# Filler matmuls from a table, and a new order of all work, in attention with a two-layer block

## The chip, the cores and the metric

The kernel runs on one core of one Trainium2 chip. The metric is the time of one execution in device microseconds, as the median of several runs. Five engines work side by side and wait for each other by semaphores: TensorE (PE), VectorE (DVE), ScalarE (ACT), GpSimd (POOL) and SyncE (SP), which issues most of the transfers.

## What is computed

Attention with a band and block sums (4 batches, 8 heads, 768 rows, 64 columns), and on its output a two-layer block over 3,072 rows (512 to 2,048 to 512):

```python
k_sum = k.reshape(B, H, nb, block, D).max(axis=3)      # block = 32
v_sum = v.reshape(B, H, nb, block, D).mean(axis=3)
scores_l = scale * np.matmul(q, k.transpose(0, 1, 3, 2))
mask_l = np.abs(pos[:, None] - pos[None, :]) < window   # window = 16
scores_s = scale * np.einsum('bhsd,bhnd->bhsn', q, k_sum) + np.log(block)
...
a = a / (np.sum(a, axis=-1, keepdims=True) + 1e-09)
return np.matmul(a, np.concatenate([v, v_sum], axis=2))
# then, on x = the heads side by side:
h = x @ w_in
g = h - np.tanh(h)
return g @ w_out
```

## The kernel before

The rows are cut into eight units `u` of 384 rows (two to a batch), the heads into two groups `g` of four. For a unit and a group the work runs: loads of k, q and v; turns of k and q on VectorE into `kT` and `qT`; block maxima of k (`top`) and their copy between the keys (`top put`); block means of v by matmuls (`sum`), copied out and put among the v rows by transfers (`mean put`); `scores` on TensorE; for each pair of heads a softmax (`min` on VectorE, `exp` on ScalarE, `inverse`, `normal`); turns of the probabilities on TensorE (`p turn`) and their copies out (`p out`); `values`; and then the layers: `in`, the activation (`tanh`, `square`, `series`, `g`, split into `g high` and `g low`), `out`. Weights come as 64-bit numbers and are converted by VectorE and ScalarE (`w scale` to `w sign`). The probabilities lie in three buffers (`PROBS`, line 24), so the next pair's `min` waits for turns of the pair before.

Every piece of work is a task of a `Plan`. The plan has 3,628 tasks with a number each. `ORDER` (line 29) is a list of these numbers, found by a search beforehand, that fixes the order in which all tasks are issued, and so each engine's own order. `ON` (line 32) is a letter for each task that tells its engine where several could do it (D, A, P, S; T for TensorE). `Plan.follow` walks through ORDER, books each task on its engine with a written-out cost, and follows TensorE's clock by a small model (`Clock`).

`follow` also puts in fillers. A filler is a matmul of the 128x128 identity by itself that nobody reads (`keep_warm`, near the end of `program`); it occurs as two records in the trace. Where the plan expects TensorE to wait, it fills the expected gap with fillers of a booked cost of 0.111 us:

```python
while spot < 2 and now - free[PE] > 2 * cost + 0.1:
    d = Task()
    d.after, d.order, d.go, d.engine, d.start = (), (), go[spot], PE, free[PE]
    d.out = free[PE] = clock.run(free[PE], cost)
```

`spot` is 0 up to the second scores (the fillers write the bank `pY2`), 1 from the first values to the third scores (they write `pS0`), and 2 later: no fillers. An engine works its tasks strictly in order, so whatever stands behind a filler on TensorE waits for it. The start of TensorE's order is: sum 0, sum 1, scores 0, p turn 0 to 2, scores 1 (the second group of the same unit, from the buffers `wg3` and `oo`), p turn 3 to 5, values 0, the first steps of `in`, and so on to scores 2, the next unit's.

Of the kernel before, what the change touches and what calls it, by code (L numbers as in the profile page):

```python
# [1335 lines left out]
```

## Time and profile before

| | us |
|---|---|
| median of 3 runs | 671.39 |
| lowest and highest | 670.67, 675.03 |
| the profiled execution | 673.41 |
| its span, first to last instruction | 671.7 |

The profile's page gives the busy time of each engine, its share of the span, a chain of waits followed back from the last instruction, and the costliest groups of instructions. Nearly all instructions are recorded by one helper, so they all have line 55, and the tiles' names tell them apart: `ident` by `ident` is a filler, `kT,qT` into four banks are scores (`wg,oo` the second group's), `ident,prob` are probability turns, `probT,vw` values, `o,wf` the first layer, `gh` by `wf`, `wh` or `wl` into `pY` the second. PEclk is the granted TensorE clock, in tenths of full speed in the page and as a fraction in the windows; the DMA share is the mean busy share of 16 DMA engines. Matmuls are pipelined, so the sum of their durations can be longer than the time they take together, and a few records can be missing.

### The profile page before, as it was taken

To read this page: it belongs to the slowest core of one execution; us is meant where nothing else is said; L and a number is where in the kernel's file an instruction comes from. 1 tells how busy PE (TensorE), PEld (TensorE's weight loads), DVE (VectorE), ACT (ScalarE), POOL (GpSimd) and SP (SyncE) were. 2 spreads that over 40 slices of the span, in tenths; PEclk is the share of its full clock that TensorE was granted. 3 is DMA by queue.
4 is the path that set the end of the run, shared out by engine and by line. 5 is a ranking of instruction groups with operands and counts; after the bars stand their busy time and mean duration, and the time that the engine had idled before them with its cause. 6 is when DMAs were issued, how large, how long until landed. Compare 5 with 4: busy or idle time off the path is not lost.

```text
span 671.7 us, 15484 instructions
## 1 busy us (share of the span) xinstructions
PE 650.4 (97%) x5471; PEld 551.4 (82%) x5471; DVE 450.6 (67%) x1272; ACT 453.6 (68%) x1371; POOL 158.6 (24%) x253
## 2 busy tenths in 40 slices
PE   6999999999799999999999999999999999999997
PEld 6986556678688889988888789989888899999885
DVE  2369899999699775545667894545678863354553
ACT  2169789899698885545588975446598855434774
POOL 2001130104400431331335501322233301000231
PEclk9999999999899999999999999999999999999999
DMA  7737887764686678757625246646553045554101
GB/s 201 191 109 215 226 241 228 195 212 140 190 292 243 213 241 225 235 170 204 201 64 179 74 144 202 199 143 207 158 149 104 22 147 178 177 167 161 47 1 50
DMA packets 120737, 113.26 MB, mean 169 GB/s; under 512 B 45008, under 2 KB 88528, under 8 KB 120656
## 3 DMA queue, kind: packets, MB, share of 16 engines
q1 hardware_dynamic: 116752, 109.61, 53.7%
q10 hardware_dynamic: 3904, 2.62, 1.3%
q8 instruction: 44, 0.72, 0.5%
q14 instruction: 37, 0.30, 0.1%
HBM read 88.87 MB, written 20.97 MB: 164 GB/s over the span
## 4 chain that ended last, share of the span: by engine, by line
PE 68%; DVE 9%; DMA 8%; ACT 6%; POOL 3%; issue 2%; SPq 2%; ACTq 0%; DVEq 0%; POOLq 0%
PE pY L55 34%; PE pH L55 29%; PE pS L55 3%; PE pX L55 2%; DVE tmp L55 2%; DVE wraw L55 2%; SPq L55 2%; ACT prob L55 2%; POOL tmp L55 2%; DMA wraw<-scr 2%; DMA tmp<-in_v_dram 1%; DMA raw<-in_k_dram 1%; DVE prob L55 1%; DMA raw<-in_q_dram 1%; ACT o L55 1%
## 5 line engine op out<-in xcount | busy, mean ns | idle before, releaser
L55 ACT ACTIVATE prob<-prob,stat 128x120 f32<-128x120 f32 x301 | 110.9, 387 | 46.5 <-DVE stat L55 45.8
L55 PE MATMUL pY<-wl,gh 128*128 128x512 f32 x288 | 113.3, 393 | 0.0
L55 PE MATMUL pH<-wf,wraw 128*128 128x384 f32 x552 | 112.4, 338 | 0.9 <-DMA wraw<-scr 0.7
L55 PEld LDWEIGHTS pH<-wf,wraw 128*128 128x128 f32 x552 | 97.4, 188 | 6.9 <-issue 1.4
L55 PE MATMUL pH<-wg,wraw 128*128 128x384 f32 x432 | 85.9, 339 | 1.4 <-DVE o L55 0.9
L55 PE MATMUL pY<-wh,gh 128*128 128x512 f32 x204 | 83.1, 408 | 0.0
L55 PE MATMUL pY<-wh,gl 128*128 128x512 f32 x204 | 80.7, 396 | 0.0
L55 PEld LDWEIGHTS pH<-wg,wraw 128*128 128x128 f32 x432 | 75.7, 188 | 5.9 <-DVE o L55 1.4
L55 PE MATMUL pY<-wg,gh 128*128 128x512 f32 x168 | 69.1, 411 | 0.0
L55 PE MATMUL pH<-o,wf 128*128 128x384 f32 x188 | 66.0, 445 | 2.7 <-DVE wf L55 1.6
L55 ACT ACTIVATE gu<-gu 128x384 f32<-128x384 f32 x128 | 65.6, 520 | 2.0
L55 PE MATMUL pY<-wg,gl 128*128 128x512 f32 x168 | 66.7, 397 | 0.0
L55 PEld LDWEIGHTS pY<-wl,gh 128*128 128x128 f32 x288 | 54.2, 188 | 9.3 <-issue 0.2
L55 POOL TENSOR_TENSOR gl<-gu,gh 128x384 fp32r<-128x384 f32 x28 | 29.2, 1043 | 120.8 <-ACT gh L55 78.9
L55 ACT ACTIVATE gt<-gu 128x384 f32<-128x384 f32 x48 | 25.0, 520 | 39.1 <-DVE gu L55 37.3
L55 PEld LDWEIGHTS pH<-o,wf 128*128 128x128 f32 x188 | 34.6, 191 | 17.9 <-ACT gu L55 1.5
L55 ACT ACTIVATE gv<-pH 128x384 f32<-128x384 f32 x37 | 18.1, 489 | 40.8 <-PE pH L55 40.8
L55 PEld LDWEIGHTS pY<-wh,gl 128*128 128x128 f32 x204 | 38.2, 187 | 8.7
L55 PE MATMUL pY<-wf,gh 128*128 128x512 f32 x108 | 44.8, 439 | 0.0
L55 POOL TENSOR_TENSOR gu<-gu,gt 128x384 f32<-128x384 f32 x24 | 24.4, 1019 | 83.6 <-ACT gu L55 60.6
L55 PEld LDWEIGHTS pY<-wh,gh 128*128 128x128 f32 x204 | 38.4, 188 | 7.0 <-issue 0.3
L55 DVE COPY gv<-pH 128x384 f32<-128x384 f32 x35 | 19.5, 556 | 34.1 <-PE pH L55 34.0
(211 smaller groups left out, 1435.5 us busy)
## 6 DMA issues: line engine op xcount, KB each, us to landing
wraw<-scr SPq DMA_DIRECT2D x72, 512.0 KB
wraw<-in_moe_w_in_dram SPq DMA_DIRECT2D x16, 512.0 KB
wraw<-in_moe_w_out_dram SPq DMA_DIRECT2D x16, 512.0 KB
scr<-wraw SPq DMA_DIRECT2D x16, 512.0 KB
wraw<-scr SPq DMA_DIRECT2D x24, 256.0 KB
raw<-in_q_dram SPq DMA_DIRECT2D x54, 96.0 KB
vw<-in_v_dram SPq DMA_DIRECT2D x60, 80.0 KB
raw<-in_k_dram SPq DMA_DIRECT2D x48, 96.0 KB
```

The lines of the kernel that those rows point to most:

```text
L55: return lambda *args, **kwargs: self._tc.keep_in_program_order(op(*args, **kwargs))
```

## The change

A table `FILL` says before which task how many fillers stand, 37 in all; the old rule for gaps stays only as the branch without a table, and there fills 0.55 of a gap. The cost that is booked for a filler goes from 0.111 to 0.223 us, the rate booked for loads of q and k from 260 to 240 thousand bytes per us. ORDER and ON are replaced as a whole by another searched order. The work itself, its tasks and its buffers are the same.

```diff
-ORDER = [15, 13, 14, 16, 1, 45, 17, 24, 18, 6, 0, 9, 27, 29, 28,
...
+ORDER = [48, 15, 16, 13, 17, 19, 27, 14, 22, 30, 11, 29, 28, 10,
...
-ON = 'PPAPAPPDDPPPPSSSSAASADSSASDSSASDDPSSSSSSSSSSSSSSSAASSDASAADAAAADDDSSSS
...
+FILL = {125: 7, 133: 2, 154: 10, 158: 1, 190: 11, 262: 1, 217: 4, 286: 1}
+ON = 'PPAPAPPDDPPPPSSSSSASSDSASSDAAASDDASSSSSSSSSSSSSSSSSAADSAASDAASSDDDSSSS
...
-                while spot < 2 and now - free[PE] > 2 * cost + 0.1:
+                for _ in range(FILL.get(t.index, 0) if FILL is not None else int(0.55 * (now - free[PE]) / cost) if spot < 2 and now - free[PE] > 0.4 else 0):
                     d = Task()
-                    d.after, d.order, d.go, d.engine, d.start = (), (), go[spot], PE, free[PE]
+                    d.after, d.order, d.go, d.engine, d.start, d.behind = (), (), go[spot], PE, free[PE], t
...
-        cost = nbytes / 260e3 if kind in ("q load", "k load") else fixed_part + nbytes / rate
+        cost = nbytes / 240e3 if kind in ("q load", "k load") else fixed_part + nbytes / rate
...
-    for t in plan.schedule((0.111, [keep_warm(tag) for tag in warm])):
+    for t in plan.schedule((0.223, [keep_warm(tag) for tag in warm])):
```

The numbers in FILL are tasks: 125 is sum 1, 133 scores 0, 154 p turn 0, 158 p turn 2, 190 scores 1, 262 a step of the first layer, 217 values 2 and 286 scores 2.

Read by engine, the two lists compare so: 406 tasks change engine, among them `g` (28 from VectorE to GpSimd, 20 the other way), `g low` (20 and 16), `part`, `g high`, `normal` and copies between VectorE and ScalarE, 10 loads of q and k from ScalarE's queue to SP's and 7 the other way. TensorE has the same 743 tasks in both.

## Rows read from the trace of the kernel before

**Rows 1.** The page's first part: busy us, share of the span, instructions.
```profile
PE 650.4 (97%) x5471; PEld 551.4 (82%) x5471; DVE 450.6 (67%) x1272; ACT 453.6 (68%) x1371; POOL 158.6 (24%) x253
```

**Rows 2.** TensorE's groups by form: busy us, mean ns, idle before. The fillers.
```profile
L55 PE MATMUL pY<-ident 128*128 128x128 f32 x252 | 32.6, 293 | 4.2 <-POOL ident L55 4.2
...
L55 PE MATMUL pS<-ident 128*128 128x128 f32 x30 | 4.1, 278 | 0.0
```

**Rows 3.** Windows: busy us and instructions per engine, clock, DMA share, GB/s.
```profile
core 0: us, PE busy (x) PEld busy (x) DVE busy (x) ACT busy (x) POOL busy (x), PEclk, DMA share, GB/s
0.00:43.00 43.00, 37.88 (x489) 36.33 (x494) 17.55 (x51) 14.48 (x57) 6.34 (x32) 1.00 0.68 183
43.00:60.00 17.00, 15.96 (x234) 12.14 (x223) 14.44 (x54) 13.37 (x48) 0.91 (x2) 1.00 0.50 148
60.00:101.00 41.00, 38.11 (x394) 22.87 (x394) 37.00 (x108) 34.31 (x115) 11.20 (x12) 1.00 0.84 233
...
168.00:335.00 167.00, 161.31 (x1367) 142.97 (x1366) 114.17 (x330) 113.20 (x347) 48.25 (x79) 0.99 0.71 223
```

**Rows 4.** The chain of waits by line: 0 to 62, then 56 to 102 us.
```profile
by line: PE pY L55 51.0%; DMA gu<-in_v_dram 8.4%; PE pH L55 7.4%; DMA raw<-in_k_dram 6.5%; SPq L55 5.3%; DVE prob L55 4.8%; DVE tmp L55 4.3%; PE pS L55 3.4%; issue 3.0%; PE pX L55 2.6%; DVE wf L55 2.1%; DVE stat L55 1.0%; DVE o L55 0.8%; DV
...
by line: DMA raw<-in_k_dram 18.7%; SPq L55 12.8%; DMA raw<-in_q_dram 12.6%; ACT prob L55 10.9%; DMA wraw<-in_moe_w_out_dram 10.8%; issue 6.8%; DVE kT L55 4.3%; ACT tmp L55 3.9%; DVE tmp L55 3.3%; ACT wh L55 2.5%; DVE qT L55 2.4%; ACT gu L55
```

**Rows 5.** Timeline, TensorE: start, us, work, idle before with its releaser.
```profile
8.97 11.06 PE L55 MATMUL pY<-ident 128*128 128x128 f32 x76
...
20.78 2.05 PE L55 MATMUL pY<-ident 128*128 128x128 f32 x16
22.76 0.31 PE L55 MATMUL pH<-kT,qT 32*64 32x120 f32 x1
...
24.32 9.42 PE L55 MATMUL pY<-ident 128*128 128x128 f32 x82
33.58 0.60 PE L55 MATMUL pS<-ident,prob 128*120 128x128 f32 x4
...
34.99 7.53 PE L55 MATMUL pY<-ident 128*128 128x128 f32 x66
42.45 0.31 PE L55 MATMUL pH<-wg,oo 32*64 32x120 f32 x1
...
59.15 1.05 PE L55 MATMUL pS<-ident 128*128 128x128 f32 x8
```

**Rows 6.** Timeline, VectorE, the work that TensorE's next step needs.
```profile
15.32 0.98 DVE L55 STREAM_TRANSPOSE qT<-wg 128x768 f32<-128x768 f32 x1 [1.81 <-DMA wg<-in_q_dram]
...
28.11 0.40 DVE L55 TENSOR_SCALAR prob<-prob,stat 128x120 f32<-128x120 f32 x1
...
38.05 0.36 DVE L55 COPY wg<-wg 128x384 f32<-128x384 f32 x1
```

**Rows 7.** Windows inside the first 43 us.
```profile
0.00:3.00 3.00, 0.00 (x0) 0.00 (x0) 0.00 (x0) 0.00 (x0) 1.92 (x11) 1.00 0.29 76
9.00:14.00 5.00, 5.00 (x25) 5.00 (x25) 3.65 (x4) 1.38 (x8) 0.34 (x1) 1.00 0.94 248
...
38.00:42.00 4.00, 4.00 (x38) 4.00 (x37) 2.36 (x7) 2.58 (x7) 0.45 (x1) 1.00 0.05 14
```

**Rows 8.** The tile ident on TensorE: least, median, longest ns.
```profile
L55 PE MATMUL pY<-ident x252: 275/275/583, 4.2 to 42.2; 128*128 128x128 f32 x126
```

**Rows 9.** GpSimd and VectorE by form: the same two operations on each.
```profile
L55 POOL TENSOR_TENSOR gl<-gu,gh 128x384 fp32r<-128x384 f32 x28 | 29.2, 1043 | 120.8 <-ACT gh L55 78.9 <-DVE gh L55 38.4 <-PE pH L55 2.9
L55 POOL TENSOR_TENSOR gu<-gu,gt 128x384 f32<-128x384 f32 x24 | 24.4, 1019 | 83.6 <-ACT gu L55 60.6 <-DVE gh L55 19.8 <-ACT gt L55 3.1
...
L55 DVE TENSOR_TENSOR gu<-gu,gt 128x384 f32<-128x384 f32 x52 | 29.8, 576 | 6.2 <-ACT gu L55 6.2
L55 DVE TENSOR_TENSOR gl<-gu,gh 128x384 fp32r<-128x384 f32 x48 | 28.4, 592 | 4.5 <-ACT gh L55 3.7
```

**Rows 10.** TensorE's waits by releaser: total us, times, longest us.
```profile
PE pY L55 <- POOL ident L55: 4.2, 1, 4.2
```

More of the change, by code (lines that the diff above doesn't have):

```diff
@@ L32 @@
-ON = 'PPAPAPPDDPPPPSSSSAASADSSASDSSASDDPSSSSSSSSSSSSSSSAASSDASAADAAAADDDSSSSSSSSSSSSDDDDSADDDSADDDSDDDDSDDDDSADDDSADDDSADDDTAAAASSSTDDDDSSSTDDDDDDAAAAAADDAAPADPTATATATDDDDDDDAAAAAAPDAAAADATDTDTATATDDDDDDAAAAAAPDADPADATATATDTADDDDDDAAAAAADDDDAADDTATATATATTTTADAAAPSSSSDTTTTADAAAPSSSSSSSSSSSSSSTDDDDDDAAAAAADDDDAAAATATATATADDDDDDDAAAAAADDAPPAAATDTATATADTTTADTADAAAPSSSSTAAAATTTADTDDAAAPSSSSDSSSSDDASSSSDSSSSDTTTADSADDDTADAAAPSSAADTTTADSADDDTADAAAPAPSSSSSSSSSSSSSSTDDDDDDAAAAAADDAAADAPTATATATADDDDDDDAAAAAADDAAAAAATATATATADSADDDAPTTTSADDDTADAAADAPSSSSTAAAASADDDADTTTSADDDTADAAADADSADDDADTTTSADDDTADAAADADSADDDADTTTSADDDTADAAADADSADDDADTTTSADDDTADAAADADSADDDADTTTSADDDTADAAADAPSSSSSSSSSSSSSSTDDDDDDAAAAAADDDDDDAAAADATATATATADDDDDDAAAAAADDPDDDPAADAATATATATDSADDDADTTTSADDDTADAAAPADSDDDDADTTTSDDDDTDDAAADADSADDDADTTTSADDDTADAAADADSADDDADTTTSADDDTADAAADADSADDDADTTTTAAAPDDSSSSSSSSSSSSSSTDDDDDDAAAAAADDDDPDAPAPPATATATATADDDDDDAAAAAADDDDDDAAAAAATDTDTDTASADDDAPTTTASASASTAAADAPSSSSDSSSSDDASSSSDSSSSDTTTTAAADADSPSPSPSPTTTTAAADAPTTTTAAADAPTTTTAAADSSSSDDDDDDADSADSADSSSSSSSSSSSSSSTDDDDDDAAAAAADDPDDDAAAAAATATATATADDDDDDAAAAAAPDDDDDAAAAAATATATATATTTTAAADSSSSDDDDDDADSADSADTATTTTAAADSSSSDDDPDDADSADSADTTTTAAADSSSSDDDDDDADSADSAPTTTTAAADSSSSDDDDDDADSADSADSSSSSSSSSSSSSSTDDDDDDAAAAAADDDDDDAAAAAATATDTATADDDDDDAAAAAADDDDDDAAAAAATATATATATTTTAAADSSSSDDDDDDADSADSADTTTTAAADSSSSDDDDDDADSADSADSPSPSPSPTTTTAAADSSSSDDDDDDADSADSADTTTTAAADADTTTTAAADADTTTTAAADADTASSSSDSSSSDDASSSSDSSSSDTTTADADDDADADADDDDDDDDPADADAPADADADAPADSSSTTADTATTADSTDTDAAAPADTTTASAAASAAADAPTTTSSSTTDDTATTADSTATDAAAPDPSSSSSSSSSSSSSSTDDDDDDAAAAAADDPDDDPAPDPATATATATADDDDDDAAAAAADDDDDDAPPAPPTDTATDTDTTTAAAPAPTTTSSSTTADTDTTADSTDTDAAAPDPTTTAAADDPTTTSSSTTDDTDTTDDSTDTDAAAPDDTTTAAAPDDTTTSSSTTADTATTADSTATDAAADAPTTTAAADDDSSSSSSSSSSSSSSTDDDDDDAAAAAAPDPDDDAAAADPTATATATDDDDDDDAAAAAADDPDDDDADPAPTDTATATATTTSSSTTDDTDTTDDSTATDAAADDDSSSSDSSSSDDDSSSSDSSSSDTTTAAAPAPSPSPSPSPTTTSSSTTADTDTTDDSTDTDAAADADTTTAAADDDTTTSSSTTDDTATTADSTDTDAAAPAPTTTAAADDDTATTTAAADDDTTTASASASAAAPDDSSSSSSSSSSSSSSTDDDDDDAAAAAADDPDDDPPAPAPTDTATDTADDDDDDAAAAAAPDPDDDPDADDATDTDTATDTTTAAADAPTTTAAADDDTTTAAADDPTTTAAADDDTTTAAADDDTTTAAADADTTTAAADADSSSSSSSSSSSSSSTDDDDDDAAAAAADDDDPDAPPDPPTDTDTDTDDDDDDDAAAAAAPDPDDDPDAAAATATATDTATTTAAAPDDSPSPSPSPTTTAAADADTTTAAAPADTTTAAADDPTTTAAADADTATTTAAADADTTTAAADADSSSSDSSSSDDPSSSSDSSSSDTTTADDDADAPADADDDDDDDDDADADADAPDDADADADSSSTTDDTATTADSTATDAAADDDTTTASASASAAADADTTTSSSTTDDTDTTDDSTDTDAAAPDDSSSSSSSSSSSSSSTDDDDDDAAAAAAPDPDPDPPADAATATDTDTADDDDDDAAAAAAPDDDDDDAAPDATATATATDTTTAAAPDPTTTSSSTTDDTATTDDSTATDAAAPDPTTTAAAPDDTTTSSSTTDDTDTTADSTDTDAAAPDDTTTAAAPDPTTTSSSTTDDTATTADSTDTDAAAPDPTTTAAADAPSSSSSSSSSSSSSSTDDDDDDAAAAAAPDDDPDPADPDATATDTATDDDDDDDAAAAAADDPDDDDAPDAATATDTATATTTSSSTTADTATTADSTDTDAAAPADSSSSDSSSSDDPSSSSDSSSSDTTTAAADDPTTTSSSTTDDTATTADSTATDAAADAPTTTAAADDPTTTSSSTTDDTDTTADSTATDAAADDDTTTAAADDPTTTAAADDPTTTASAAASAAADDPSSSSSSSSSSSSSSTDDDDDDAAAAAADDPDDDPADDPPTATATDTADDDDDDAAAAAADDDDDDPPPADDTDTATATATTTAAADDDTTTAAADDDTTTAAADDPTTTAAADDDTTTAAAPDDTTTAAAPADTTTAAAPADSSSSSSSSSSSSSSTDDDDDDAAAAAADDPDDDDDPADATDTDTDTADDDDDDAAAAAADDPDDDAPDPADTATDTATDTTTAAADDPTTTAAADADTTTAAADDDTTTAAADADTTTAAADDPTTTAAADADTTTAAADADTTTADDDADADDDADDDDDPDDDADADDPDPDDDDDDADSSSTTADTATTADSTATDAAADADTTTASASASAAADADTTTSSSTTDDTATTDDSTATDAAADAPTTTAAADDDTTTSSSTTADTDTTADSTATDAAAPDDTTTAAADDPTTTSSSTTADTATTDDSTATDAAADADTTTAAADDDTTTSSSTTDDTATTADSTATDAAADADTTTAAAPDDTTTSSSTTADTDTTDDSTDTDAAADDDTTTAAADDDTTTSSSTTDDTDTTDDSTATDAAAPADTTTAAADDDTTTSSSTTADTDTTDDSTDTDAAAPDPTTTAAADDDTTTAAADADTTTAAASASAAADADTTTAAAPDDTTTAAADDDTTTAAAPDDTTTAAAPADTTTAAAPDDTTTAAADADTTTAAADDPTTTAAAPDDTTTAAAPDPTTTAAADDDTTTAAAPDDTTTAAAPDDTTTAAAPADTTTAAADDDTTTDDTTTAAASAASSDTD'
@@ new lines @@
+FILL = {125: 7, 133: 2, 154: 10, 158: 1, 190: 11, 262: 1, 217: 4, 286: 1}
+ON = 'PPAPAPPDDPPPPSSSSSASSDSASSDAAASDDASSSSSSSSSSSSSSSSSAADSAASDAASSDDDSSSSSSSSSSSSDDDDSADDDSADDDSADDDSADDDSDDDDSADDDSADDDTAAAASSSTDADDSSSTDDDDDDAAAAAADDDAPDAATATATATDDDDDDDAAAAAAPDADAAAATATATDTDTDDDDDDAAAAAADDDPPAAPTATATDTADDDDDDAAAAAADDDDAADDTATATATATTTTADAAAPSSSADTTTTDDAAAPSSSSSSSSSSSSSSTDDDDDDAAAAAAPDAAAADATATATATADDDDDDDAAAAAADDAAAPAATATATATADTTTADTADAAAPSSSSTAAAATTTADTADAAAPSSSSDSSSSDDASSSSDSSSSDTTTADSDDDDTADAAAPSSASDTTTADSADDDTADAAAPAPSSSSSSSSSSSSSSTDDDDDDAAAAAADDAAADAPTATATATADDDDDDDAAAAAADDAAAAAATATATATADSADDDAPTTTSDDDDTADAAADAPSSSSTAAAASADDDADTTTSADDDTADAAADADSADDDADTTTSADDDTADAAADADSADDDADTTTSADDDTADAAADADSADDDADTTTSADDDTADAAADADSADDDADTTTSADDDTDDAAADAPSSSSSSSSSSSSSSTDDDDDDAAAAAADDPDDDAAAAAATATATATADDDDDDAAAAAAPDDDDDADAAAATATATATASADDDADTTTSADDDTADAAAPADSDDDDADTTTSDDDDTADAAADADSDDDDADTTTSADDDTADAAADDDSADDDADTTTSADDDTADAAAPDDSADDDADTTTTAAAPADSSSSSSSSSSSSSSTDDDDDDAAAAAAPDDDDDDDDAAATATDTATADDDDDDAAAAAADDDDDDAAAAAATATATDTASADDDADTTTASASASTAAADADSSSSDSSSSDDASSSSDSSSSDTTTTAAADADSPSPSPSPTTTTAAADAPTTTTAAADAPTTTTAAADSSSSDDDDDDADSADSADSSSSSSSSSSSSSSTDDDDDDAAAAAADDPDPDAAAAAATATATATADDDDDDAAAAAAPDDDDDAAAAAATATATATATTTTAAADSSSSDDDDDDADSADSADTATTTTAAADSSSSDDPDDDADSADSADTTTTAAADSSSSDDDDDDADSADSAPTTTTAAADSSSSDDDDDDADSADSADSSSSSSSSSSSSSSTDDDDDDAAAAAADDPDDDAAAAAATDTDTDTADDDDDDAAAAAADDDDDDAAAAAATDTATATATTTTAAADSSSSDDDDDDADSADSADTTTTAAADSSSSDDDDDDADSADSADSPSPSPSPTTTTAAADSSSSDDDDDDADSADSADTTTTAAADADTTTTAAADADTTTTAAADADTASSSSDSSSSDDDSSSSDSSSSDTTTADADADADADADDDDDDDDDADADADADADADADADSSSTTADTATTADSTATDAAADADTTTASASAAAAADDDTTTSSSTTDDTDTTADSTATDAAAPDPSSSSSSSSSSSSSSTDDDDDDAAAAAAPDDDDDPPDDPPTDTDTDTADDDDDDAAAAAAPDDDPDPPDPDATATDTATATTTAAAPADTTTSSSTTDDTDTTDDSTATDAAADDPTTTAAAPAPTTTSSSTTDDTDTTDDSTDTDAAADAPTTTAAAPDPTTTSSSTTDDTDTTADSTATDAAAPDPTTTAAAPAPSSSSSSSSSSSSSSTDDDDDDAAAAAAPDDDPDAAAADDTATDTDTADDDDDDAAAAAAPDDDPDPAPAAATDTDTATDTTTSSSTTDDTATTDDSTATDAAAPDPSSSSDSSSSDDASSSSDSSSSDTTTAAADADSPSPSPSPTTTSSSTTADTATTADSTATDAAAPAPTTTAAAPDDTTTSSSTTADTDTTDDSTATDAAADDPTTTAAADDDTATTTAAADDDTTTASASASAAADDDSSSSSSSSSSSSSSTDDDDDDAAAAAADDDDDDPAADDDTATDTATDDDDDDDAAAAAADDPDDDADAAAATATATATATTTAAADDDTTTAAADDDTTTAAAPDPTTTAAAPDDTTTAAAPDDTTTAAADDDTTTAAADADSSSSSSSSSSSSSSTDDDDDDAAAAAADDDDDDDDDADATATDTDTDDDDDDDAAAAAADDPDDDAAAPAATATATATATTTAAADADSPSPSPSPTTTAAADADTTTAAADDDTTTAAADDPTTTAAAPADTATTTAAADADTTTAAADADSSSSDSSSSDDPSSSSDSSSSDTTTDPAPDDDDADADPDDDDDDDADADDDADDPADAPDDSSSTTDDTDTTDDSTDTDAAADADTTTASASASAAAPADTTTSSSTTADTDTTADSTATDAAAPADSSSSSSSSSSSSSSTDDDDDDAAAAAAPDPDPDDPPPDPTATDTATDDDDDDDAAAAAAPDPDDDPPDPPDTATDTATDTTTAAAPAPTTTSSSTTADTATTADSTATDAAADDDTTTAAAPDPTTTSSSTTADTATTADSTATDAAAPDDTTTAAADAPTTTSSSTTDDTDTTDDSTDTDAAAPDPTTTAAAPDDSSSSSSSSSSSSSSTDDDDDDAAAAAADDPDDDPDDPDDTDTDTATDDDDDDDAAAAAAPDDDPDDDPPADTATDTATDTTTSSSTTADTDTTDDSTATDAAAPAPSSSSDSSSSDDPSSSSDSSSSDTTTAAAPDPTTTSSSTTDDTDTTADSTDTDAAADADTTTAAADDDTTTSSSTTADTDTTADSTATDAAAPAPTTTAAAPDDTTTAAADDDTTTASAAASAAADDDSSSSSSSSSSSSSSTDDDDDDAAAAAAPDDDPDPADDDPTATATATDDDDDDDAAAAAADDDDDDAPAPDPTATATATATTTAAADDPTTTAAAPDPTTTAAADDPTTTAAADDDTTTAAADDDTTTAAAPDDTTTAAADDDSSSSSSSSSSSSSSTDDDDDDAAAAAAPDDDPDDPADPDTATDTDTADDDDDDAAAAAADDDDDDPADADATATDTDTATTTAAAPAPTTTAAADDDTTTAAADDDTTTAAADDDTTTAAAPADTTTAAADADTTTAAADDDTTTADDDAPDPADADPDPPDDDPADADDPDDADADDPADSSSTTDDTATTDDSTDTDAAADAPTTTASAAASAAAPAPTTTSSSTTDDTATTDDSTATDAAAPADTTTAAAPDPTTTSSSTTADTATTDDSTDTDAAAPADTTTAAADDDTTTSSSTTADTDTTDDSTATDAAADADTTTAAAPDDTTTSSSTTDDTDTTADSTATDAAAPDDTTTAAADDDTTTSSSTTDDTATTADSTATDAAAPAPTTTAAADDDTTTSSSTTDDTATTADSTDTDAAADDDTTTAAAPAPTTTSSSTTADTDTTDDSTATDAAAPADTTTAAAPDDTTTAAAPDDTTTASAAASAAADDPTTTAAADDPTTTAAADDPTTTAAAPDDTTTAAADDDTTTAAADDDTTTAAADDDTTTAAADDPTTTAAAPDDTTTAAADDPTTTAAADDDTTTAAAPDDTTTAAADAPTTTAAADDPTTTAAADADTTTDDTTTAAASAASSDTD'
```

2 lines of the change are left out of this document (1 added, 1 removed).

## The prediction

> **What bounds the kernel now.** I read the page's busy shares first. TensorE is busy for 97% of the span, VectorE and ScalarE for two thirds [rows 1]; the reader is to ask what that busy time is. The groups by form answer: 252 + 30 = 282 matmul records of `ident` by `ident` are fillers, two to a filler, so 141 fillers, and they take 32.6 + 4.1 = 36.7 us [rows 2]. The 97% hides work that computes nothing.
>
> Then the windows. In the first 43 us TensorE is busy for 37.9 us, while VectorE and ScalarE work for 17.6 and 14.5 us and the DMA share is 0.68; from 60 to 101 us VectorE is at 37.0 of 41 us and the DMA share is at 0.84; from 168 us on TensorE is at 161.3 of 167 us [rows 3]. So there are a start, a middle stage that is tight on transfers and VectorE, and a long stage bound by TensorE. The chain of waits tells which work of the start counts: of the first 62 us, matmuls into `pY`, the fillers' bank there, hold 51%. Between 56 and 102 us transfers lead: loads of k, of q and of a weight, 18.7, 12.6 and 10.8% [rows 4]. A shorter start therefore meets the transfers next.
>
> The timeline puts a time to it, each as "ready" against "started".
> - First scores: the last input, the turned q, is there at 15.32 + 0.98 = 16.3 us [rows 6]. They start at 22.76, behind 76 and 16 filler records (38 and 8 fillers) [rows 5]: 6.4 us late.
> - First probability turn: its probabilities are ready at 28.11 + 0.40 = 28.5 us [rows 6]; it starts at 33.58, behind 41 fillers [rows 5]: 5.1 us late.
> - Second scores: the key sums are put by 38.05 + 0.36 = 38.4 us [rows 6]; they start at 42.45, behind 33 fillers [rows 5]: 4.0 us late. In the meantime the DMA engines stand: share 0.05 from 38 to 42 us [rows 7].
>
> Sum: 15.5 us in which nothing but fillers holds the chain. The cause can be read off too: the planner booked 0.111 us for a filler; 82 records in 9.42 us are 0.23 us each [rows 5]. 141 x 0.111 = 15.7 us were booked and 36.7 were taken.
>
> **The change part by part.** Fillers. The table keeps 7 before the second mean sum, 2 before the first scores, 10 before the first probability turn, 1 before the third, 11 before the second scores, and 1 + 4 + 1 later. I place them by the rows. The 7 start at 8.97 us; from 9 to 14 us 25 filler records took 5.0 us [rows 7], 0.40 us for a filler, so they end at 8.97 + 2.8 = 11.8 us, and the inputs of the first scores come at 16.3: hidden, and so are the 2. The 10 take 2.3 us (0.23 each) against 24.3 to 28.5, 4.2 us of waiting: hidden, even at 0.40 each. The 11 take 2.5 us; between the third turn's end (about 35.0, where the 66 records begin) and the sums at 38.4 lie 3.4 us: hidden. If the cover were gone, all 30 of these would cost at most 30 x 0.40 = 12 us. So the whole 15.5 us come free. Of 15 fillers between 47 and 60 us 6 stay; the 4 at 59.15 take 1.05 us [rows 5] just ahead of the third scores. The others mostly wait with their neighbours: I take 0.5 us back (0 to 2).
>
> TensorE's clock. The granted clock reads 1.00 from 9 to 14 us, yet a filler took 0.40 us there and 0.23 later, and the same record needs 583 ns at the longest, 275 at the median [rows 7, 8]. TensorE thus began at the lower of its levels (1.2 GHz), and rose to 2.4 after running fillers without a break. With 7 fillers there it may rise later. Price: the second mean sum (from the 76 records' end at 20.0 to 20.78, 0.8 us), the scores (22.76 to 24.32, 1.6), three turns (some 0.8) and the second scores (1.6), doubled at the most: 0 to 4.8 us. I take 1.0, nearer to nothing: from the first scores on TensorE is nearly without a gap again, and matmuls at the lower level fill their gaps better. The Trainium skill (TensorE: Matmul & The Clock Gate, "What's actually happening") says that the throttled level is the default and that activity releases it. By that rule alone the change would give up to the whole 4.8 us back here, 663 us, and the second rival is where it goes on for longer; the trace agrees as far as the longest filler shows it.
>
> Transfers. What is late next is the DMA. To 101 us it has moved 0.68 x 43 + 0.50 x 17 + 0.84 x 41 = 72.1 us of full work [rows 3]. In the first 3 us the share is 0.29 [rows 7], 0.9 us of work; the other 71.2 at the best long share seen, 0.84, need 84.8 us. So what ends at 101 us can end at 87.8: a gain of 13.2 us at most by this rate. Bounds: at 0.94, as from 9 to 14 us [rows 7], it caps nothing (71.2 / 0.94 = 75.7 + 3, 22 us); at today's mean, 72.1 / 101 = 0.71, the gain is nothing.
>
> Order. By ORDER and ON, 406 of 3,628 tasks change engine. TensorE keeps all its 743 tasks; on average one moves by 2 places, at most by 14, and the first 13 stand as they were. DMA issues move most: on SP's queue by 8 places on average (stores to scratch by up to 129); 10 loads of q and k go from ScalarE's queue to SP's and 7 the other way. On SP they queue behind mean puts that wait for the mean sums, which now come sooner; on ScalarE one load of q waits behind a copy of the first mean. For the second scores one load of k stands behind the first exponentials, as before. GpSimd goes from 190 tasks to 201. I see no row that shows the new order to stall more or less, and take 0. Bounds: TensorE stands idle for 5.7 us of 168 to 335 us [rows 3], of which a better order could win some 4; a worse one can cost as much again. The longer step for a filler (0.223) and the slower rate for q and k only change what is planned.
>
> Sum along the chain: 15.5 + 0.5 - 1.0 = 15.0 us; the transfers let 13.2 through. The profiled execution took 673.4 us (span 671.7, and 1.7 around it), 2.0 above the median, and the gain lies wholly within the span: 673.4 - 13.2 = 660.2 there, **658 us** as a median (671.4 - 13.2).
>
> **The rivals.**
> - The transfers cap it lower. For: the chain from 56 to 102 us runs through loads, and 0.84 was reached only there [rows 3, 4]; each part of the start that moves up has its own waits for buffers. Against: the DMA stands at 38 to 42 us [rows 7], which the change removes. At a share of 0.76: 71.2 / 0.76 + 3 = 96.7, a gain of 4.3 us, 667 us.
> - TensorE stays at its lower level. Its work without fillers up to 60 us is 37.9 + 16.0 - 36.7 = 17.1 us [rows 2, 3]; all of it doubled, in place of the 1.0 us taken, gives 658 + 16 = 674; half of that, 666. Against: after 43 us TensorE is busy for 16.0 of 17 us, with 4 us of fillers in it.
> - Slower: GpSimd. 48 products and low parts of the activation (28 `g`, 20 `g low`) move there from VectorE; one takes 1.04 or 1.02 us there, 0.59 or 0.58 on VectorE [rows 9], 0.45 longer. If TensorE waited for each, 48 x 0.45 = 21.6 us: 680 us. It decides for slower by over 1% from (678.1 - 658.2) / 0.45 = 44 of the 48. Against: TensorE waits for GpSimd once, for `ident` at the start [rows 10], and 36 such tasks go the other way.
> - The order is worse all along and eats the gain: in the range.
>
> **How the numbers follow.** The forecast's mechanism 0.72, with 650 to 664 of its own (15.5 + 2 us without any cap, and 4 from the order, make 650); the cap 0.13 (664 to 670); the lower level 0.07; GpSimd 0.06; others 0.02. The range of 650 to 668 takes in the cap's 667 and half of the second rival. A change of 1%, 6.7 us, is about what a measurement can tell here. Under 664.7: the forecast and a fifth of the cap, 0.75. Over 678.1: GpSimd and the worst of the rest, 0.07. Between: 0.18.
>
> **What would show it.** Right: 74 filler records of about 9 us; first scores near 16.5 to 18 us, first probability turn some 4 us after they end, second scores near 27 to 30 us; no window like 38 to 42 us; a DMA share of 0.8 or more over the first 88 us; the stage from 168 us on shifted forward as a whole. Wrong: second scores late because a load of k lands late (the cap); the real matmuls of the first 40 us at double length (the lower level); waits of TensorE for GpSimd; or more idle time of TensorE behind 168 us than 6 us, which would be the order.

## The result

| | before | changed |
|---|---|---|
| median, us | 671.66 (20 runs) | 665.75 (20 runs) |
| lowest and highest, us | 668.19, 675.03 | 660.16, 670.6 |
| the profiled execution, us | 673.41 | 665.20 |
| its span, us | 671.7 | 663.5 |

The ratio is 0.9907, with a 95% interval of 0.9886 to 0.9927: faster by 0.93%, 6.2 us (4.9 to 7.7). It leaves out the two of the 20 runs that lie more than 1.5% above the fastest; the medians of all runs are 5.9 us apart. The forecast was 13 us faster, 658, with 650 to 668 as the range. So the time lies in the range and the sign is right, but under half of the gain came, and less than the 1% that the chances called faster.

The page of the changed kernel answers to [rows 1]: engine, busy us, share, records, and the granted clock in 40 slices.

```profile
PE 630.3 (95%) x5263; PEld 527.6 (80%) x5263; DVE 444.0 (67%) x1267; ACT 452.2 (68%) x1365; POOL 171.4 (26%) x264
...
PEclk9889999999999999999999999999999999999999
```

TensorE's groups by form answer to [rows 2]:

```profile
L56 PE MATMUL pY<-ident 128*128 128x128 f32 x62 | 10.1, 325 | 0.0
...
L56 PE MATMUL pS<-ident 128*128 128x128 f32 x12 | 1.9, 283 | 0.0
```

74 records, 37 fillers, in 10.1 + 1.9 = 12.0 us in place of 36.7. TensorE is busy for 20 us less, and the span is 8.2 us shorter: 12 us of what the fillers held came back as waits. The windows answer to [rows 3] (span; busy us and records of TensorE, its weight loads, VectorE, ScalarE, GpSimd; clock; DMA share; GB/s):

```profile
0.00:43.00 43.00, 25.70 (x427) 21.21 (x428) 24.19 (x82) 21.81 (x83) 6.17 (x33) 0.92 0.76 201
43.00:60.00 17.00, 16.27 (x194) 10.05 (x193) 15.22 (x48) 14.31 (x50) 2.32 (x3) 1.00 0.74 221
60.00:101.00 41.00, 37.82 (x324) 22.73 (x324) 38.81 (x99) 36.01 (x114) 9.34 (x9) 1.00 0.78 223
168.00:335.00 167.00, 163.63 (x1473) 145.10 (x1470) 118.02 (x346) 115.09 (x346) 49.52 (x80) 1.00 0.68 211
```

The reader is to see three things. VectorE and ScalarE did 24.2 and 21.8 us of work in the first 43 us, 17.6 and 14.5 before, so the start did move up. The DMA share rose from 0.68 to 0.76 and from 0.50 to 0.74, but between 60 and 101 us it fell from 0.84 to 0.78. And the clock in the first 43 us is 0.92.

The timeline of TensorE answers to [rows 5]: the fillers, the first probability turns, and p turn 3.

```profile
10.79 3.03 PE L56 MATMUL pY<-ident 128*128 128x128 f32 x14
...
14.56 0.71 PE L56 MATMUL pY<-ident 128*128 128x128 f32 x4
...
16.79 2.50 PE L56 MATMUL pY<-ident 128*128 128x128 f32 x20
23.60 1.11 PE L56 MATMUL pS<-ident,prob 128*120 128x128 f32 x4 [4.31 <-DVE prob L56]
...
25.72 3.23 PE L56 MATMUL pY<-ident 128*128 128x128 f32 x22
...
34.53 1.11 PE L56 MATMUL pX<-ident,prob 128*120 128x128 f32 x4
```

The second scores began here:

```profile
28.88 0.31 PE L56 MATMUL pH<-wg,oo 32*64 32x120 f32 x1
```

### The profile page after: what moved, and what is told of

Read it like the earlier page. It is cut to its first block, busy times and chain, and to the rows that moved or that the text cites. A ratio compares the mean times of both kernels' runs of the same rounds, so it can differ in the third digit from the quotient of the medians.

```text
span 663.5 us, 15046 instructions
## 1 busy us (share of the span) xinstructions
PE 630.3 (95%) x5263; PEld 527.6 (80%) x5263; DVE 444.0 (67%) x1267; ACT 452.2 (68%) x1365; POOL 171.4 (26%) x264
## 4 chain that ended last, share of the span: by engine, by line
PE 68%; DMA 11%; DVE 10%; ACT 4%; issue 3%; SPq 2%; POOL 1%; ACTq 0%; DVEq 0%; POOLq 0%
PE pH L56 31%; PE pY L56 31%; PE pS L56 4%; DMA wraw<-in_moe_w_in_dram 3%; PE pX L56 2%; DVE tmp L56 2%; DVE wf L56 2%; DMA wraw<-in_moe_w_out_dram 2%; DMA wraw<-scr 2%; SPq L56 2%; DMA raw<-in_q_dram 1%; DMA raw<-in_k_dram 1%; ACT prob L56 1%; DMA tmp<-in_v_dram 1%; DVE gl L56 1%
## 5 line engine op out<-in xcount | busy, mean ns | idle before, releaser
L56 ACT ACTIVATE prob<-prob,stat 128x120 f32<-128x120 f32 x299 | 109.5, 385 | 39.3 <-DVE stat L56 38.5
L56 POOL TENSOR_TENSOR gu<-gu,gt 128x384 f32<-128x384 f32 x35 | 36.6, 1050 | 119.8 <-ACT gu L56 114.9
L56 ACT ACTIVATE gv<-pH 128x384 f32<-128x384 f32 x33 | 16.2, 490 | 45.4 <-PE pH L56 45.2
L56 DVE COPY gv<-pH 128x384 f32<-128x384 f32 x39 | 21.7, 556 | 33.6 <-PE pH L56 33.6
L56 ACT ACTIVATE gu<-pH 128x384 f32<-128x384 f32 x49 | 23.7, 486 | 22.7 <-PE pH L56 19.0
```

The source lines that it names most:

```text
L56: return lambda *args, **kwargs: self._tc.keep_in_program_order(op(*args, **kwargs))
```

## Where the gain went, step by step

The table holds the starts of TensorE's milestones, in us, from the timelines of the two executions.

| | before | changed | earlier by |
|---|---|---|---|
| first scores | 22.76 | 15.28 | 7.5 |
| first probability turn | 33.58 | 23.60 | 10.0 |
| second scores | 42.45 | 28.88 | 13.6 |
| p turn 3, first of the second pair | 43.98 | 34.53 | 9.5 |
| third scores (next unit) | 60.13 | 50.72 | 9.4 |
| fourth scores | 87.87 | 79.10 | 8.8 |
| fifth scores | 123.94 | 115.64 | 8.3 |
| last matmul of the second layer | 666.68 | 658.46 | 8.2 |

So the loss lies in the start, above all between the second scores and p turn 3; behind it the gain shrinks by 1.3 us and then goes through to the end. The forecast for p turn 3 can be settled like an account. By the rows of before, it was 6.4 + 5.1 us late for the first scores and the first turn, and 3.7 for itself (its last probability was normalised at 40.3 us, it started at 43.98): 15.2 us. The first scores did better by 1.1 us. Four items were lost:

**VectorE's line, 2.6 us.** From the first scores to the first turn it took 23.60 - 15.28 = 8.3 us; the rows of before gave 5.7 (22.76 to ready at 28.5). VectorE in the changed kernel, behind the last minimum of the first pair (start, us, work, idle before with its releaser):

```profile
17.98 0.28 DVE L56 CUSTOM_DVE_ANT_0 prob<-pS,mask 128x120 f32<-128x120 f32 x1
...
20.99 0.43 DVE L56 TENSOR_SCALAR tmp<-wraw 128x512 f32<-128x512 f32 x1 [2.71 <-DMA wraw<-in_moe_w_in_dram]
...
22.94 0.60 DVE L56 TENSOR_SCALAR prob<-prob,stat 128x120 f32<-128x120 f32 x2
```

It stood for 2.71 us for the load of the first weight, and only then came the steps of the softmax that the turn waits for. In the kernel before, the same conversion stood at the same place of VectorE's line, but there it began at 25.71 us without a wait: the fillers had kept the scores back until the weight was there.

**The clock, 0.5 us.** TensorE's waits show a stop of 4.3 us ahead of the first turn, behind the ten fillers (16.79 to 19.3), and one of 2.7 us that the profile can't name:

```profile
PE pS L56 <- DVE prob L56: 4.5, 2, 4.3
PE pH L56 <- issue: 2.7, 1, 2.7
```

The granted clock fell to 0.5 at 23.6 us, after the first of these, and again at 33.8, after the second. The three turns took 1.68 us from first to third in place of 1.16.

**The softmax of the second pair, 0.7 us**, from the third turn to the last normalisation (6.2 us, 5.5 before).

**A stop in the midst of the second scores, 3.0 us.** The probabilities for p turn 3 were ready at 31.5 us, but TensorE was not through with the scores in front of it. Of the 3.0 us, 2.4 are the stop, which began at 31.27 us, and 0.6 are the last scores behind it, at the lower clock. The last rows ahead of the stop and the first behind it:

```profile
30.97 0.29 PE L56 MATMUL pY<-wg,oo 32*64 32x120 f32 x3
33.93 0.45 PE L56 MATMUL pH<-wg,oo 32*64 32x120 f32 x1 [2.66 <-issue]
```

TensorE had begun the scores (at 28.88 us, with a short wait for the block sums of k before 29.87) and waited for no data that the profile shows; 89 of their 96 matmuls were done. 15.2 + 1.1 - 2.6 - 0.5 - 0.7 - 3.0 = 9.5 us, as measured.

The rest is the base. The execution of before that is compared here lay 1.75 us above its kernel's median, and the changed kernel's lies 0.55 below: 8.2 us between the spans are 5.9 between the medians.

## The experiments

All ratios are to the kernel before, run beside on the same chip, with 95% intervals. The fillers are counted in the traces. Each run has a profile of one of its executions only, so a time in a trace belongs to that one execution.

| | order | fillers | median, us | ratio |
|---|---|---|---|---|
| e2 | new | 128, the old rule | 671.21 | 0.9992 (0.9969 to 1.0016) |
| changed | new | 37 | 665.75 | 0.9907 (0.9886 to 0.9927) |
| e5 | new | 37 | 666.31 | 0.9913 (0.9882 to 0.9945) |
| e1 | old | 37 | 662.92 | 0.9877 (0.9841 to 0.9912) |
| e6 | old | 37 | 666.33 | 0.9907 (0.9875 to 0.9939) |
| e3b | new, one weight later | 37 | 665.53 | 0.9901 (0.9866 to 0.9937) |
| e4 | new | 45 | 664.06 | 0.9895 (0.9866 to 0.9925) |
| e11 | new, one weight later | 47 | 664.47 | 0.9875 (0.9848 to 0.9902) |
| e7 | old | 52 | 663.20 | 0.9864 (0.9834 to 0.9893) |
| e10 | new | 55 | 664.01 | 0.9881 (0.9844 to 0.9919) |
| e9 | old | 62 | 660.70 | 0.9831 (0.9797 to 0.9865) |
| e8 | new | 0 | 662.46 | 0.9864 (0.9824 to 0.9904) |
| e12 | old | 0 | 662.20 | 0.9840 (0.9819 to 0.9860) |

### Fillers or order? e1, e2 and e6

e1 puts the table into the kernel before and leaves its ORDER and ON; e6 is the same kernel once more, with more rounds.

```diff
 ORDER = [15, 13, 14, 16, 1, 45,
...
+FILL = {125: 7, 133: 2, 154: 10, 158: 1, 190: 11, 262: 1, 217: 4, 286: 1}
...
-                while spot < 2 and now - free[PE] > 2 * cost + 0.1:
+                for _ in range(FILL.get(t.index, 0)):
...
-    for t in plan.schedule((0.111, [keep_warm(tag) for tag in warm])):
+    for t in plan.schedule((0.223, [keep_warm(tag) for tag in warm])):
```

> The kernel before with its own ORDER and ON, and only the fillers of the change: the table with 37, in place of the rule with 141. Filler theory (the overrun of the fillers is all of the gain, the order gives nothing): 665 to 667 us, as the changed kernel; first scores near 17 us, first probability turn near 23 to 24 us, second scores near 29 us. Order theory (the new order carries the gain, as it moves loads and turns too): 669 to 672 us, with the second scores kept beyond 32 us by loads that the old order issues too late.

> The old order with the table of 37 once more, with more rounds. Theory that the new order costs time: 2 to 4 us less than the changed kernel on the same chip, 662 to 664 us. Rival (the orders are alike): within 1 us of the changed kernel, 665 to 666 us.

e2 is the changed kernel, its new ORDER and ON, with the old rule and the old booked cost.

```diff
 ORDER = [48, 15, 16, 13, 17, 19,
...
-                for _ in range(FILL.get(t.index, 0) if FILL is not None else int(0.55 * (now - free[PE]) / cost) if spot < 2 and now - free[PE] > 0.4 else 0):
+                while spot < 2 and now - free[PE] > 2 * cost + 0.1:
...
-    for t in plan.schedule((0.223, [keep_warm(tag) for tag in warm])):
+    for t in plan.schedule((0.111, [keep_warm(tag) for tag in warm])):
```

> The changed kernel with its new ORDER and ON, but with the old rule for fillers and the old booked cost of 0.111 us. Filler theory: 670 to 673 us, the gain is gone; some 120 to 150 fillers, and the first probability turn and the second scores 4 to 12 us later than in the changed kernel (23.60 and 28.88 us). Order theory: 664 to 668 us.

e2 gave 671.21 us: with the old rule the gain is gone, whatever the order. Its groups by form show 256 filler records in 32.9 us, and its timeline 38 fillers ahead of the first probability turn and 38 ahead of the second scores, much as before (41 and 33):

```profile
L56 PE MATMUL pY<-ident 128*128 128x128 f32 x208 | 26.5, 291 | 0.0
...
L56 PE MATMUL pS<-ident 128*128 128x128 f32 x48 | 6.4, 279 | 0.0
```

```profile
20.93 8.75 PE L56 MATMUL pY<-ident 128*128 128x128 f32 x76
...
30.93 8.65 PE L56 MATMUL pY<-ident 128*128 128x128 f32 x76
```

The first turn and the second scores came at 29.52 and 39.51 us, 5.9 and 10.6 later than in the changed kernel, as forecast.

e1 gave 662.92 us and e6 666.33: the table alone, in the old order, gives all of the gain. The filler theory holds, and e1's first scores, first turn and second scores (16.23, 23.76 and 29.07 us) came as it said. Whether the new order costs something can't be told from these: e1 lies below the changed kernel, e6 beside e5 doesn't, so the 2 to 4 us that e6's theory named did not come. With no filler at all (e8 and e12, below) the orders differ by 0.3 us in their medians and by 1.6 in their ratios, inside both intervals. In all five pairs of runs with like fillers (e6 and e5, e1 and the changed kernel, e12 and e8, e7 and e4, e9 and e10) the old order has the lower ratio, by 0.0006 to 0.005. No pair is clear by itself, so a cost of the new order is neither shown nor excluded.

### The stop in the second scores: e5, and e1 against e6

e5 is the changed kernel once more.

> The changed kernel once more, beside the next run on the same chip. Theory that TensorE lacks its instructions in the second scores (it stood 2.66 us in the midst of them, from 31.27 us, for nothing that the profile shows, while the DMA share was 1.02): the same stop at the same matmul of the second scores, 2 to 3 us long. Rival (an accident of one execution): no stop there. Time 665 to 666 us.

The stop was there again, at the same matmul, the 89th of the second scores, 1.8 us long. It was not an accident of one execution. e6 has it too, 3.15 us, between these rows:

```profile
30.54 0.32 PE L56 MATMUL pY<-wg,oo 32*64 32x120 f32 x3
34.01 0.31 PE L56 MATMUL pH<-wg,oo 32*64 32x120 f32 x1 [3.15 <-issue]
```

e1, the same program as e6, doesn't have it; the second scores run straight into p turn 3:

```profile
30.38 0.29 PE L56 MATMUL pY<-wg,oo 32*64 32x120 f32 x3
30.60 0.82 PE L56 MATMUL pX<-ident,prob 128*120 128x128 f32 x4
```

Counted from the start of the trace, TensorE's stop comes behind its 705th record (matmuls, weight loads and waits) in the changed kernel, in e5, in e6 and in e3b below, in both orders. That points to a fixed place in TensorE's own program and not to data. The trace has the transfers of the queue named "instruction". In the changed kernel one of 16 KB begins at 31.2 us, as TensorE stops, in 2 us in which the DMA share is at or above 1 (queue, packets, MB, share of 16 engines):

```profile
q8 instruction: 1, 0.02, 3.7%
```

In e1 it comes at 20.8 us, long before it is needed:

```profile
q8 instruction: 1, 0.02, 2.8%
```

So I read the stop as TensorE out of instructions: the next block comes late. Two more facts of the traces bear this out. The queue's packets go with TensorE's records, 42 for 10,598 of them in e8 and 44 for 11,169 before, about 250 to a packet. And in all four profiles with the stop TensorE goes on 1.4 to 1.6 us after the packet has come in, wherever the stop began (us):

| | packet | TensorE stands |
|---|---|---|
| changed | 31.23 to 32.41 | 31.27 to 33.93 |
| e5 | 30.61 to 31.60 | 31.39 to 33.17 |
| e6 | 31.14 to 32.59 | 30.86 to 34.01 |
| e3b | 28.47 to 29.66 | 29.27 to 31.11 |

That full queues hold the packet up is not shown: it takes 1.0 to 1.5 us here and 1.2 in e1, and in the changed kernel the DMA share is down to 0.34 from 33 to 34 us, where TensorE still stands. A part of what makes it late can be read off. With 37 fillers TensorE stands ahead of the first probability turn behind its 465th to 467th record. With 45 to 62 it passes that place before it stands, and the packet begins at 18.8 to 20.6 us, at record 458 to 507. So I read it that the table of 37 puts the wait just where the packet falls due, and that e1 and e6 fell on two sides of it. What then holds the packet back until 28 to 31 us stays open. The Trainium skill (Runtime: NRT & Kernel Launch, "Instruction fetch mechanics") says that instructions come in blocks of 16 KiB, fetched while the block before runs, and that the cost of crossing into the next is mostly hidden. The size agrees with the packet; in four of the five profiles with 37 fillers it is not hidden but costs 1.8 to 3.2 us. In the seven profiles with no filler or with 45 to 62, no stop of 1 us or more is in the second scores. With 45 to 62 the packet is early; with none it is as late (32.2 us in e8, 30.5 in e12), but the 705th record comes only at 36 to 37 us.

### The clock: e4, e8, e12

e4 fills the wait ahead of the first turn.

```diff
-FILL = {125: 7, 133: 2, 154: 10, 158: 1, 190: 11, 262: 1, 217: 4, 286: 1}
+FILL = {125: 7, 133: 2, 154: 18, 158: 1, 190: 11, 262: 1, 217: 4, 286: 1}
```

> The changed kernel with 18 fillers in place of 10 before the first probability turn, so that the 4.31 us in which TensorE stands there (19.29 to 23.60 us) are filled. Theory that the clock's fall at 23.58 us costs time: no granted clock of 0.5 there, the first three probability turns take 1.2 us in place of 1.7 from the first to the third, second scores 0.3 to 0.8 us earlier, 665 us. Rival (the fall is free, as the second scores wait for their keys): the same times, 665.7; and if the fillers overrun, the first probability turn comes later than 23.60.

The first turn stood at 23.65 us, so the eight more cost nothing; the three turns took 1.21 us, as forecast. The clock did not fall at 23.6, but at 25.2 us. The second scores came at 29.28 us, 0.4 later and not 0.3 to 0.8 earlier. p turn 3 came at 30.98 us, 3.55 earlier than in the changed kernel, nearly all of it because the stop in the second scores was gone: the packet had come at 19.7 us. At the fifth scores 1.9 us were left (113.72 against 115.64), in the medians 1.7, which the intervals don't separate. The theory was right on the turns and not on what they are worth.

e8 and e12 take all fillers away, in the new order and in the old.

```diff
-FILL = {125: 7, 133: 2, 154: 10, 158: 1, 190: 11, 262: 1, 217: 4, 286: 1}
+FILL = {}
```

> The changed kernel with no filler at all. Theory that the 37 keep the clock: the granted clock rises later or falls more often before 60 us, the first scores and probability turns take twice as long, 667 to 671 us. Rival (with 37 the clock falls anyway, they buy nothing): 665 to 666 us.

> The old order with no filler at all, beside the new order with none (662.46 us). Theory that the new order costs time: 659 to 661 us. Rival (the orders are alike): 662 to 663.5 us.

e8 gave 662.46 us, below both of its expectations, and e12 662.20, as its rival said; the runs of each lie within 1.2 us. The windows of e8 show that the clock is indeed lower (columns as above):

```profile
20.00:27.00 7.00, 1.74 (x6) 0.98 (x6) 5.76 (x20) 4.36 (x18) 0.39 (x1) 0.55 0.61 162
27.00:34.00 7.00, 5.11 (x108) 4.12 (x110) 5.36 (x20) 4.92 (x19) 0.25 (x1) 0.50 0.89 224
```

and the turns of the probabilities take 421 ns at the median in e8, up to 34 us, and in e12 up to 31 us; the least in e12 is 272, what they take at 2.4 GHz (operation, count, least / median / longest ns):

```profile
L56 PE MATMUL pS<-ident,prob x8: 421/421/442, 23.3 to 33.3; 128*120 128x128 f32 x8
```

```profile
L56 PE MATMUL pS<-ident,prob x8: 272/421/466, 23.1 to 31.7; 128*120 128x128 f32 x8
```

Yet e12 has its second scores at 27.32 us, 1.6 earlier than the changed kernel. In the start TensorE waits for VectorE, ScalarE and loads; at half its clock its steps are still shorter than these waits: in e12 it is busy for 11.9 of the first 31 us. The clock that the fillers keep there is worth nothing that these runs can measure. Without the fillers of the kernel before, the second scores come 15 us earlier (42.45 before), and 9 to 10 us of that are in the median.

### VectorE's line: e3b and e11

e3b moves the first weight's conversion; e3, another placing of the same steps, gave no result.

```diff
 # ORDER, by tasks
-min (first pair) x6, w scale 0, w shift 0, w low 0, sum guard 0, inverse 0, normal x2, w sign 0, min (second pair) x6, ... inverse 1, w scale 1 (ScalarE)
+min (first pair) x6, sum guard 0, inverse 0, normal x2, min (second pair) x6, ... inverse 1, w scale 0, w shift 0, w low 0, w sign 0, w scale 1 (ScalarE)
```

> The changed kernel with the four steps that convert the first weight moved in ORDER from between the first minima and the first inverse to behind the second pair's normalisation, with the next weight's scaling and the first weight's split on ScalarE behind them. Theory that VectorE's line waits for that weight's load (it stands 2.71 us for it, up to 20.99 us): first probability turn near 21 us in place of 23.60, second scores 1 to 2 us earlier than 28.88, 663 to 664.5 us. Rival (the loads of k set the second scores, whatever stands in VectorE's line): first probability turn earlier, second scores still at 28 to 29 us, the time unchanged.

The edit does not do quite what the expectation says: the four steps stand behind the second pair's inverse, but still ahead of the last piece of its normalisation on VectorE. VectorE's wait in the first pair is gone; it goes from the exponentials straight to the normalisation:

```profile
20.61 0.17 DVE L56 TENSOR_SCALAR stat<-stat 128x6 f32<-128x6 f32 x1 [1.46 <-ACT prob L56]
...
21.04 0.60 DVE L56 TENSOR_SCALAR prob<-prob,stat 128x120 f32<-128x120 f32 x2
```

The first turn came at 21.70 us (23.60) and the second scores at 26.72 (28.88), so the rival was wrong on the keys: they were there. It was right on the time. But the stop was there too,

```profile
PE pH L56 <- issue: 1.8, 1, 1.8
```

and the fourth scores came at 80.03 us, 0.9 later than in the changed kernel. The time is the same, 665.53 us, where 663 to 664.5 were forecast. e11 takes the stop away as well, with 20 fillers for 10 ahead of the first turn.

> The changed kernel with the first weight's conversion behind the second pair's normalisation and 20 fillers in place of 10 before the first probability turn: two of the losses named in the start (VectorE's line, the stop in the second scores) taken away at once. If these losses are what the forecast lacked: no stop in the second scores, p turn 3 at 28 to 30 us in place of 34.53, 661 to 663 us. Rival (the middle stage takes back whatever the start gains beyond some 11 us, as without the fillers): p turn 3 as early as that, but the fourth scores (79.10 us in the changed kernel) not before 76 us, 663 to 665 us.

p turn 3 began at 29.91 us, 14.1 earlier than before: nearly all of the 15.2 of the account. But the fourth scores came at 79.91, 8.0 earlier, and the time was 664.47: the rival was right on the times. Not all of the 6.1 us went to the middle stage. Only the first matmul of p turn 3 ran at 29.91; the next waited for VectorE, whose last normalisation now stood behind the moved conversion (28.40 to 30.70 us):

```profile
31.80 0.28 DVE L56 TENSOR_SCALAR prob<-prob,stat 128x120 f32<-128x120 f32 x1
...
32.13 0.85 PE L56 MATMUL pX<-ident,prob 128*120 128x128 f32 x3 [1.90 <-DVE prob L56]
```

Before, that second matmul ran at 44.14 us, so 12.0 us were left there, and e11 moved the loss in VectorE's line more than it took it away. The execution profiled also lies 2.4 us above e11's median. The windows of e11:

```profile
0.00:43.00 43.00, 29.50 (x454) 24.32 (x454) 25.66 (x88) 22.53 (x88) 6.17 (x33) 0.92 0.75 196
43.00:60.00 17.00, 15.59 (x188) 10.10 (x189) 15.11 (x42) 15.03 (x48) 2.24 (x3) 1.00 0.87 242
60.00:101.00 41.00, 36.92 (x295) 22.51 (x294) 36.70 (x95) 33.62 (x107) 8.97 (x9) 0.96 0.75 211
```

From 60 to 101 us the DMA share is 0.75, no better than in the changed kernel; a weight whose conversion starts later holds its buffer longer, and the loads behind it wait. That last step is argued from the order of the work and not tried by itself.

What becomes of the start's gain can be followed in the profiles of all kernels but e2 (us earlier than before):

| | order | p turn 3 | third scores | fourth scores |
|---|---|---|---|---|
| changed | new | 9.5 | 9.4 | 8.8 |
| e3b | new | 12.3 | 11.7 | 7.8 |
| e4 | new | 13.0 | 11.4 | 10.1 |
| e5 | new | 10.4 | 11.3 | 10.2 |
| e8 | new | 11.8 | 9.1 | 8.5 |
| e10 | new | 13.5 | 11.0 | 10.4 |
| e11 | new | 14.1 | 10.1 | 8.0 |
| e1 | old | 13.4 | 12.5 | 11.7 |
| e6 | old | 9.6 | 8.6 | 7.6 |
| e7 | old | 13.9 | 10.9 | 11.2 |
| e9 | old | 12.0 | 11.9 | 11.3 |
| e12 | old | 12.9 | 12.8 | 12.3 |

Where p turn 3 came over 11 us earlier, the new order loses 3 to 6 us of it again by the fourth scores, the old one under 3. These are single executions, and the medians don't separate the orders.

### More fillers where there is a wait: e7, e9, e10

The edits of e7 and e9 are shown against e1's table, that of e10 against the changed kernel's.

```diff
 # e7, old order
-FILL = {125: 7, 133: 2, 154: 10, 158: 1, 190: 11, 262: 1, 217: 4, 286: 1}
+FILL = {125: 12, 133: 2, 154: 20, 158: 1, 190: 11, 262: 1, 217: 4, 286: 1}
 # e9, old order
+FILL = {125: 12, 133: 5, 154: 24, 158: 1, 190: 13, 247: 4, 262: 1, 217: 4, 286: 1}
 # e10, new order
+FILL = {125: 7, 133: 2, 154: 26, 158: 1, 190: 11, 247: 3, 262: 1, 217: 4, 286: 1}
```

> The old order with a table of 52: 12 fillers before the second mean sum and 20 before the first probability turn, in place of 7 and 10, so that the waits of 2.4 and 3.1 us that e1 left there are filled. Theory that the clock's falls cost time: no granted clock of 0.5 before 40 us, 1.5 to 3 us less than with 37, 660 to 662 us, and a smaller spread from run to run. Rival (the falls are free, or the fillers overrun): as with 37 or 1 us more.

> The old order with 62 fillers: 12, 5 and 24 before the second mean sum, the first scores and the first probability turn, 13 before the second scores, 4 before the first step of the first layer. Theory that the clock's falls and a late fetch of TensorE's instructions are what is left: no stop of 2 us or more in the second scores, fewer spans at 0.5, 660 to 663 us, as low as with 52 or lower. Rival (more fillers overrun, as with the old rule): first probability turn later than 22.93 us, 664 us or more.

> The changed kernel with its new order and 55 fillers, 26 before the first probability turn and 3 before the first step of the first layer in place of 10 and none. Theory that the filling counts and the order does not: 662 to 664 us, within 1 us of the old order filled as fully, and no stop in the second scores. Rival (the new order costs 2 us or more): 664.5 to 666 us.

e7 gave 663.20 us, above the 660 to 662 of its theory, and its clock fell all the same, at 33.9 us. e10 gave 664.01, between its theory and its rival; it has no stop, but lies 3.3 us above e9. e9 gave 660.70, the lowest of all, as forecast, though its first turn came at 25.33 us, as late as its rival said. e9 beats both kernels: 0.9831 (0.9797 to 0.9865). Its clock reads 1.000, and its windows come near to what the forecast had drawn, a DMA share of 0.78 to 0.87 through to 101 us:

```profile
core 0: 660.6 us, clock 1.000
```

```profile
0.00:43.00 43.00, 31.89 (x514) 27.39 (x514) 27.13 (x96) 22.82 (x91) 7.01 (x34) 1.00 0.78 209
43.00:60.00 17.00, 16.81 (x174) 9.97 (x171) 15.40 (x46) 15.70 (x49) 3.47 (x3) 1.00 0.87 222
60.00:101.00 41.00, 37.08 (x326) 22.79 (x324) 37.12 (x92) 34.55 (x107) 7.70 (x9) 1.00 0.83 236
```

Its fourth scores stand at 76.58 us, 11.3 earlier than before, and its median is 10.9 below. But e12, with no filler and half the clock in the start, has 662.20 us: the difference to e9 is inside the intervals, so I don't claim that the clock did it. e10 against e9 leaves 3.3 us between the orders, e8 against e12 0.3; the intervals overlap, and an order effect of up to 3 us is not excluded.

## Why the prediction was right or wrong

**What bounds the start: right.** The fillers held the chain, and their overrun was what could be won: take them away and 6 to 11 us come back, in either order; put them back in the new order (e2) and nothing is left of it. 74 records were forecast in 9 us; they took 12: the 14 records at 10.8 us needed 0.43 us a filler and the 22 at 25.7 us 0.29, where 0.40 and 0.23 were reckoned.

**Each milestone by itself: right, the sum was not.** First scores at 16.5 to 18 us, measured 15.28, as the turned q was there at 15.1 and not at 16.3; second scores at 27 to 30, measured 28.88. "First probability turn some 4 us after the scores end" was the first miss: 6.8 (16.8 to 23.6). The step that failed is the sentence "So the whole 15.5 us come free". It took the distances between the milestones from the kernel before, where the fillers had hidden two other things: a weight's load in VectorE's line (2.6 us), and the edge of TensorE's instructions (3.0 us). Both were late only against a start that had moved up: 9.5 us came free at p turn 3, not 15. I had named moved loads of q and k, and the queue they stand in, but not the load that a step of VectorE's own line waits for, though that step stands between two that I had costed.

**What is late next: the second step that failed, a term too large.** The account of the start is not all of the miss. In e4 and e10 (new order) and in e7 and e12 (old) p turn 3 came 12.9 to 13.9 us earlier, and still the ratios leave gains of 7.1, 8.0, 9.1 and 10.8 us; the forecast's 13.2 was reached by no run, 11.3 at most (e9). "So what ends at 101 us can end at 87.8" was put on transfers at a share of 0.84. The changed kernel reached 0.74 to 0.78, e9 0.78 to 0.87, and the fourth scores came 8 to 12 us earlier, never 13.2. That transfers set this stage is not shown either: VectorE, which the cap leaves out, was busy for 38.8 of the 41 us from 60 to 101 us in the changed kernel (37.0 before), and no run changed one without the other. The first rival, with a gain of 4.3 us, is nearer to the result than the forecast, but its reason alone isn't what happened.

**The lower level: the price was right, the fear was not.** 0 to 4.8 us were put down and 1.0 taken; the turns paid 0.5, and e8 and e12 show that even with no filler it costs nothing that the medians show; e12's first scores took 2.7 us, not double the 1.6 of before. The rule of the Trainium skill (TensorE: Matmul & The Clock Gate, "What's actually happening"), by which activity releases the throttled level, agrees with e8's windows: TensorE worked for 1.7 us from 20 to 27 us and for 5.1 from 27 to 34, and from 34 to 41 us the clock was back, at 0.98. That it would cost the change 4.8 us does not. The 663 us for that rule was mis-added besides: 15.5 + 0.5 - 4.8 = 11.2 us lies below the cap and gives 660.

**GpSimd: right that it does not bind.** TensorE's list of waits in the changed kernel has no row with GpSimd as the releaser, though its busy time rose from 158.6 to 171.4 us.

**The order: 0 was taken.** From 168 to 335 us TensorE stood for 3.4 us (5.7 before); from 335 to 503 us it stood for 2.0 us, 0.2 before. That e8 and e12 agree to 0.3 us supports the 0, but every pair leans against the new order, and up to 3 us stay open.

**The base.** The whole was reckoned on an execution above its median, as the text said; 2.3 us of the gap between spans and medians is that. So a part of the 13.2 us was perhaps that execution's own, and no median could give it back.

The chances, 0.75 for faster by over 1%, were too sure for a sum made of waits alone: behind a wait that is taken away stands the next one, and the rows of before did not show it.

## What to carry to other kernels

Matmuls that only keep the clock can hold back what stands behind them, and in this start, which waits for others, they bought nothing that could be measured; whether they pay where TensorE is the bound, no run here shows. Cost them in measured time, put them only into waits, and try the kernel without any first. When a wait of many microseconds is removed, don't take the next distances from the old trace; list for each engine on the chain every load that its line waits for in that stretch, and when it is issued. And a few instructions more or less ahead of a wait can decide when a block of instructions is fetched, so one profile in which a step stops without cause should be taken again before it is explained.
